# A gated recurrence and a highway layer: from running products on TensorE to a scan on VectorE, channels on the partitions

## The chip, the core and the metric

The kernel runs on one core of a Trainium2 chip. The core has a matrix engine (PE, TensorE), a vector engine (DVE, VectorE), an activation engine (ACT, ScalarE), a general engine (POOL, GpSimd) and a sync engine (SP) whose queue issues transfers. Each engine works through its own instruction list in order, and semaphores make one wait for another. SBUF is the on-chip memory of 128 partitions; PSUM is the smaller memory that TensorE writes, here eight banks of 2 KB in each partition. Sixteen DMA engines move data between HBM and SBUF. The metric is the device time in microseconds (us), as the median of the runs; less is better.

## The reference

There are B = 4 sequences of S = 6336 steps with D = 256 channels, in float32. Along a sequence each channel runs a gated recurrence; each of the 25344 results then goes through a highway layer.

```python
sig = 1.0 / (1.0 + np.exp(-f_logit))
f = lower_bound[None, None, :] + (1.0 - lower_bound[None, None, :]) * sig
i = 1.0 - f
for t in range(S):
    h = f[:, t] * h + i[:, t] * x[:, t]
    y[:, t] = h
...
H = np.maximum(x @ w_h, 0.0)
T = 1.0 / (1.0 + np.exp(-(x @ w_t + b_t)))
return (T * H + (1.0 - T) * x).astype(np.float32)
```

In the last three lines x is the recurrence's result y, with one row for each token. Each of f_logit, x and the output is 25344 x 256 float32, 25.95 MB.

## The kernel before

The kernel walks through the sequences in 50 chunks of 128 steps (the last one holds 64). A chunk has the 128 steps on the partitions and 4 x 256 = 1024 (sequence, channel) pairs along the free dimension, so 512 tokens. It is written as one straight loop body; a scheduler of the framework sets the order on each engine.

The recurrence is solved inside a chunk by products. ACT computes a Tanh of f_logit (L111), DVE turns it into f (L113, L114) and 1 - f (L120), POOL multiplies that with x (L123, the input b of the recurrence), and ACT takes the logarithm of f (L117). TensorE multiplies the logarithms with a triangular matrix of ones (L127), which sums them along the steps. ACT takes exp of the sum and of its negative (L131, L133): the product P of all f so far, and its inverse. DVE forms b/P (L136), TensorE sums it along the steps with the same triangular matrix and adds the last row of the chunk before through a one-hot matrix (L140, L143), and DVE multiplies by P (L146). This is y, with steps on the partitions. The next chunk's L143 needs this chunk's y, so the chunks form a chain.

For the highway layer the channels have to be on the partitions. TensorE transposes eight blocks of y (L153), DVE copies them out of PSUM (L154), TensorE multiplies with the two weight matrices (L164, L166), DVE takes the relu (L168), ACT a Tanh that stands for the sigmoid (L169), and DVE does the scaling and the three elementwise steps of the mix (L170, L174, L175, L177). TensorE transposes the result back (L183), DVE copies it out (L184), and POOL's queue stores it, cast from bf16 to float32 on the way (L186). The loads go through SP's queue (L107, L108), with three buffers each. The functions of ACT belong to different tables, which ACT_TABLE_LOAD rows bring in. Two of the PSUM pools hold one buffer of each tile and one holds two.

## Time and profile before

| what | value |
|---|---|
| median of 3 runs | 619.56 us (619.17 to 620.91) |
| profiled execution, span | 620.2 us |
| PE, DVE, ACT, POOL busy | 346.1, 471.4, 389.3, 165.8 us |
| ACT table loads | 95 of 1283 ns |
| HBM read, written | 52.95, 25.95 MB |
| mean granted TensorE clock | 0.674 |

The span is the time from the first to the last instruction of the one execution that the profiler recorded; that execution's own time and its span agree with the median to 0.1%. A row of the groups gives line, engine, operation, output and inputs with their shapes, the count, then after the bar the busy time and the mean duration of one in ns, and after the second bar how long the engine had been idle in front of it and which instruction ended that. A row of the timeline begins with its start and its duration in us. A row of the windows gives the stretch, its length, the busy time of PE, the weight loads, DVE, ACT and POOL with their counts, the granted TensorE clock, the share of the DMA engines and GB/s.

### The profile page before, as it was taken

The numbers are of one execution on the slowest core, as the hardware profiler recorded it, in microseconds if no ns is written. First come the engines' busy times: TensorE is split into PE (matmuls) and PEld (weight loads), VectorE is DVE, ScalarE is ACT, GpSimd is POOL, SyncE is SP. The second block draws the span as 40 slices with busy tenths as digits, with TensorE's granted clock in tenths as the row PEclk, the third lists the DMA queues.
The fourth block names the chain that finished last, engine by engine and source line by source line (L and its number), as shares of the span: only waits on it lengthen the run. The fifth ranks groups of instructions, "written<-read, shape, count | busy, mean of one in ns | idle before, by whom it ended". The sixth has DMA issues, their size and how long they took to land.

```text
span 620.2 us, 4764 instructions
## 1 busy us (share of the span) xinstructions
PE 346.1 (56%) x1473; PEld 164.6 (27%) x1498; DVE 471.4 (76%) x706; ACT 389.3 (63%) x395; POOL 165.8 (27%) x115
## 2 busy tenths in 40 slices
PE   0365545556456655645655665565565575566653
PEld 0122222222132232322323223222322232232321
DVE  1488899887887887878877877878878778766653
ACT  1976999786675675676676666666765574543010
POOL 3323354242232232223223223222322132120000
PEclk9976777776766666676676666666666666666655
DMA  8947568666646645744654564565463242122222
GB/s 151 289 135 204 136 169 234 175 181 158 136 103 146 159 102 135 165 107 106 174 126 103 148 157 101 135 157 115 108 161 87 68 100 54 34 50 52 61 40 51
DMA packets 79817, 78.69 MB, mean 127 GB/s; under 512 B 2736, under 2 KB 79792, under 8 KB 79792
## 3 DMA queue, kind: packets, MB, share of 16 engines
q1 hardware_dynamic: 52576, 51.91, 32.7%
q0 software_dynamic: 27216, 26.48, 19.1%
q8 instruction: 11, 0.18, 0.1%
q14 instruction: 14, 0.11, 0.1%
HBM read 52.95 MB, written 25.95 MB: 127 GB/s over the span
## 4 chain that ended last, share of the span: by engine, by line
PE 33%; issue 27%; DVE 18%; ACT 18%; DMA 2%; POOL 1%; SPq 0%; POOLq 0%; another core or an unknown queue 0%; ACTq 0%; DVEq 0%
PE H_ps L164 10%; PE T_ps L166 9%; ACT L117 6%; ACT lf L117 5%; PE Su_ps L140 5%; DVE yT L154 4%; PE Su_ps L143 4%; DVE out_pp L184 3%; DMA flg<-in_f_logit_dram 2%; ACT T_sb L169 2%; PE Lp_ps L127 2%; ACT invP L131 2%; DVE tmp L175 2%; DVE imf L120 2%; PE tps L183 1%
## 5 line engine op out<-in xcount | busy, mean ns | idle before, releaser
L123 POOL TENSOR_TENSOR bb<-imf,xt 128x1024 bf16<-128x1024 f16 x50 | 122.1, 2442 | 310.4 <-issue 288.6
L169 ACT ACTIVATE T_sb<-T_ps,bt_sb 128x512 bf16<-128x512 f32 x100 | 68.7, 687 | 172.6 <-PE T_ps L166 172.6
L164 PE MATMUL H_ps<-yT,wh_sb 128*128 128x512 bf16 x177 | 99.0, 576 | 77.8 <-DVE yT L154 76.4
L183 PE MATMUL tps<-ident,out_dp 128*128 128x128 bf16 x400 | 44.4, 278 | 151.6 <-DVE out_dp L177 151.6
L166 PE MATMUL T_ps<-yT,wt_sb 128*128 128x512 bf16 x200 | 110.3, 564 | 6.6 <-issue 5.1
L168 DVE TENSOR_SCALAR H_sb<-H_ps 128x512 bf16<-128x512 f32 x100 | 69.0, 690 | 48.8 <-PE H_ps L164 38.4
L113 DVE TENSOR_TENSOR ftile<-sig,nlb_tile 128x1024 f16<-128x1024 f16 x50 | 64.4, 1288 | 27.6 <-ACT lf L117 22.2
L183 PEld LDWEIGHTS <-out_dp 128*128 128x128 bf16 x400 | 32.6, 125 | 180.7 <-DVE out_dp L177 180.7
L186 POOL DMA_DIRECT2D out_dram<-out_pp x50 | 39.8, 796 | 139.1 <-DVE out_pp L184 136.8
L111 ACT ACTIVATE sig<-flg 128x1024 f16<-128x1024 f32 x50 | 52.7, 1056 | 27.9 <-DVE ftile L113 15.7
L140 PE MATMUL Su_ps<-uu,L_tile 128*128 128x512 bf16 x100 | 60.5, 607 | 7.8 <-DVE uu L136 7.6
L117 ACT ACT_TABLE_LOAD x47 | 60.3, 1283 | 0.8
L166 PEld LDWEIGHTS <-wt_sb 128*128 128x128 bf16 x200 | 25.8, 129 | 124.9 <-issue 122.9
L131 ACT ACTIVATE invP<-Lp_ps 128x1024 bf16<-128x1024 f32 x50 | 51.1, 1021 | 10.0 <-PE Lp_ps L127 9.7
L117 ACT ACTIVATE lf<-ftile 128x1024 bf16<-128x1024 f16 x50 | 52.6, 1056 | 1.2 <-DVE ftile L114 0.7
L170 DVE TENSOR_SCALAR T_sb<-T_sb 128x512 bf16<-128x512 bf16 x100 | 32.3, 324 | 26.5 <-ACT T_sb L169 26.2
L133 ACT ACTIVATE Pt<-Lp_ps 128x1024 bf16<-128x1024 f32 x50 | 50.8, 1016 | 2.4 <-DVE y_b L146 2.4
L111 ACT ACT_TABLE_LOAD x39 | 50.0, 1283 | 1.4 <-PEq L202 0.7
L127 PE MATMUL Lp_ps<-lf,L_tile 128*128 128x512 bf16 x99 | 36.3, 451 | 23.9 <-ACT lf L117 18.7
L184 DVE COPY out_pp<-tps 128x1024 bf16<-128x1024 bf16 x50 | 34.1, 683 | 15.1 <-PE tps L183 15.1
L164 PEld LDWEIGHTS <-wh_sb 128*128 128x128 bf16 x200 | 29.1, 146 | 43.2 <-issue 42.7
L175 DVE TENSOR_TENSOR tmp<-tmp,T_sb 128x1024 bf16<-128x1024 bf16 x50 | 38.3, 766 | 1.4
(39 smaller groups left out, 467.1 us busy)
## 6 DMA issues: line engine op xcount, KB each, us to landing
flg<-in_f_logit_dram SPq DMA_DIRECT2D x49, 512.0 KB, 6.2
xt<-in_x_dram SPq DMA_DIRECT2D x49, 512.0 KB, 3.8
out_dram<-out_pp POOLq DMA_DIRECT2D x49, 512.0 KB, 6.4
lb_tile<-in_lower_bound_dram POOLq DMA_DIRECT2D x1, 256.0 KB, 10.5
flg<-in_f_logit_dram SPq DMA_DIRECT2D x1, 256.0 KB, 3.8
xt<-in_x_dram SPq DMA_DIRECT2D x1, 256.0 KB, 3.4
out_dram<-out_pp POOLq DMA_DIRECT2D x1, 256.0 KB, 2.5
wh_sb<-in_moe_w_h_dram POOLq DMA_DIRECT2D x1, 128.0 KB, 11.6
```

Source lines behind the costliest of these rows:

```text
L111: nc.scalar.activation(sig, flg.rearrange("p b d -> p (b d)"), AF.Tanh, scale=0.5)
L113: nc.vector.tensor_mul(ftile, sig, nlb_tile)
L117: nc.scalar.activation(lf, ftile, AF.Ln)
L123: nc.gpsimd.tensor_mul(bb, imf, xt.rearrange("p b d -> p (b d)"))
L131: nc.scalar.activation(invP, Lp_ps, AF.Exp, scale=-1.0)
L140: nc.tensor.matmul(Su_ps[:, h * 512 : (h + 1) * 512], L_tile, uu[:, h * 512 : (h + 1) * 512], start=True, stop=(c == 0))
L164: nc.tensor.matmul(H_ps, wh_sb[:, ki, mi * P : (mi + 1) * P], yT[:, ki, :, :], start=st, stop=sp)
L166: nc.tensor.matmul(T_ps, wt_sb[:, ki, mi * P : (mi + 1) * P], yT[:, ki, :, :], start=st, stop=sp)
L168: nc.vector.tensor_relu(H_sb[:, mi], H_ps)
L169: nc.scalar.activation(T_sb[:, mi], T_ps, AF.Tanh, scale=0.5, bias=bt_sb[:, mi : mi + 1])
L183: nc.tensor.transpose(tps2[:, b, dh, :], out_dp[:, dh, b, :], ident)
L184: nc.vector.tensor_copy(out_pp, tps2.rearrange("p b dh q -> p b (dh q)"))
```

## The change

The whole body is rewritten. The work is now cut into units: one of 4 x 192 tokens (96 partitions by eight blocks), then 24 of 1024 consecutive tokens of one sequence (128 partitions by eight blocks), taken in turn over the four sequences. Loads and stores keep rows of 1 KB.

`gate` computes u = sigmoid(-f_logit) on ACT, `product` computes u * x on POOL in four parts. `decay_pe` and `b_pe` transpose u and u * x on TensorE so that channels lie on the partitions, 128 at a time (h = 0, 1). `decay_act` forms f = 1 - (1 - lower_bound) u on ACT. `scan` is one instruction of DVE that runs the recurrence along the free dimension, `tensor_tensor_scan`, with the last column of the unit before as its start. The factor 1 - lower_bound of the input is left out there and put into the weights and into two diagonal matrices (`diag`, `ndiag`), so the y of the kernel is the reference's y without that factor.

The highway layer stays with channels on the partitions: `z_pe` and `t_act` give T, `g_pe` adds w_h's product and the negative of y in PSUM, `d_dve` takes the maximum with the negative of y (relu(H) - y), `e_dve` multiplies by T. `o_pe` multiplies y by the diagonal and e by the identity as stationary operands, both accumulated into one PSUM tile: this transposes back to tokens on the partitions and adds the residual. `o_act` copies it out on ACT in four parts, and SP's queue stores it as float32.

The loop at the end writes the order of all engines by hand, as a pipeline over units: unit n is scanned while n-1 goes through the highway layer, n-2 goes out, n+1 is gated and n+2 is loaded. PSUM holds uT and bT (one bank each, one buffer), zp and gp (two banks each, one buffer) and op (one bank, two buffers).

The removed lines are the loop printed above. The added ones, without the blank ones, the setting up of the names and the unchanged launch:

```diff
+    rest = S % (NB * P)
+    assert rest % 2 == 0 and rest // 2 <= P and B * 2 == NB
+    units = [(rest // 2, [(b, 0, b * rest, rest) for b in range(B)])]
+    for s0 in range(rest, S, NB * P):
+        for b in range(B):
+            units.append((P, [(b, s0, 0, NB * P)]))
+    NU = len(units)
+    inp = ctx.enter_context(tc.tile_pool(name="inp", bufs=3))
+    mid = ctx.enter_context(tc.tile_pool(name="mid", bufs=3))
+    ypool = ctx.enter_context(tc.tile_pool(name="ypool", bufs=6))
+    ffn = ctx.enter_context(tc.tile_pool(name="ffn", bufs=2))
+    outp = ctx.enter_context(tc.tile_pool(name="outp", bufs=2))
+    ps1 = ctx.enter_context(tc.tile_pool(name="ps1", bufs=1, space=bass.MemoryType.PSUM))
+    ps2 = ctx.enter_context(tc.tile_pool(name="ps2", bufs=2, space=bass.MemoryType.PSUM))
+    st = [dict() for _ in range(NU)]
+    def load(n):
+        np_, segs = units[n]
+        lt = inp.tile([P, NB, D], FP32, tag="lt")
+        xt = inp.tile([P, NB, D], FP32, tag="xt")
+        for src, t in ((f_logit, lt), (x, xt)):
+            if len(segs) == 1:
+                b, s0, _, ln = segs[0]
+                nc.sync.dma_start(t, src[b, s0:s0 + ln, :].rearrange("(j p) d -> p j d", p=np_))
+            else:
+                t4 = t.rearrange("p (b j) d -> p b j d", j=2)
+                for j in range(2):
+                    nc.sync.dma_start(
+                        t4[:np_, :, j, :],
+                        src[:, j * np_:(j + 1) * np_, :].rearrange("b p d -> p b d"))
+        st[n]["lt"], st[n]["xt"] = lt, xt
+    load(0)
+    load(1)
+    ident_b = singles.tile([P, P], BF16, name="ident_b")
+    make_identity(nc, ident_b)
+    ident_h = singles.tile([P, P], FP16, name="ident_h")
+    make_identity(nc, ident_h)
+    lb = singles.tile([P, NH], FP32, name="lb")
+    bt = singles.tile([P, NH], FP32, name="bt")
+    w_raw = singles.tile([P, 2, NH, D], FP32, name="w_raw")
+    for h in range(NH):
+        for vec, t in ((lower_bound, lb), (moe_b_t, bt)):
+            nc.scalar.dma_start(t[:, h:h + 1], bass.AP(
+                tensor=vec.tensor, offset=vec.offset + h * P, ap=[[1, P], [1, 1]]))
+    for k, w in enumerate((moe_w_h, moe_w_t)):
+        nc.scalar.dma_start(w_raw[:, k], w.rearrange("(h p) o -> p h o", p=P))
+    cc = singles.tile([P, NH], FP32, name="cc")
+    nc.vector.tensor_scalar(cc, lb, -1.0, 1.0, op0=ALU.mult, op1=ALU.add)
+    ncc = singles.tile([P, NH], FP32, name="ncc")
+    nc.vector.tensor_scalar(ncc, lb, 1.0, None, op0=ALU.subtract)
+    w_sb = singles.tile([P, 2, NH, D], BF16, name="w_sb")
+    diag = singles.tile([P, NH, P], FP16, name="diag")
+    ndiag = singles.tile([P, NH, P], FP16, name="ndiag")
+    for h in range(NH):
+        for k in range(2):
+            nc.vector.tensor_scalar(w_sb[:, k, h], w_raw[:, k, h], cc[:, h:h + 1], None, op0=ALU.mult)
+        nc.vector.tensor_scalar(diag[:, h], ident_h, cc[:, h:h + 1], None, op0=ALU.mult)
+        nc.vector.tensor_scalar(ndiag[:, h], ident_h, ncc[:, h:h + 1], None, op0=ALU.mult)
+    def gate(n):
+        np_, _ = units[n]
+        u = mid.tile([P, NB, D], FP16, tag="u")
+        nc.scalar.activation(u[:np_], st[n]["lt"][:np_], AF.Sigmoid, scale=-1.0)
+        st[n]["u"] = u
+    def product(n):
+        np_, _ = units[n]
+        bv = mid.tile([P, NB, D], BF16, tag="bv")
+        for q in range(0, NB, 2):
+            nc.gpsimd.tensor_mul(bv[:np_, q:q + 2], st[n]["u"][:np_, q:q + 2], st[n]["xt"][:np_, q:q + 2])
+        st[n]["bv"] = bv
+    def decay_pe(n, h):
+        np_, _ = units[n]
+        uT = ps1.tile([P, NB * P], FP16, tag="uT")
+        for j in range(NB):
+            nc.tensor.transpose(uT[:, j * np_:(j + 1) * np_], st[n]["u"][:np_, j, h * P:(h + 1) * P], ident_h[:np_, :np_])
+        st[n]["uT"] = uT
+    def decay_act(n, h):
+        np_, _ = units[n]
+        N = NB * np_
+        if h == 0:
+            st[n]["f"] = mid.tile([P, NH, NB * P], FP16, tag="f", name="f")
+        nc.scalar.activation(st[n]["f"][:, h, :N], st[n]["uT"][:, :N], AF.Identity, scale=ncc[:, h:h + 1], bias=1.0)
+    def b_pe(n, h):
+        np_, _ = units[n]
+        bT = ps1.tile([P, NB * P], BF16, tag="bT")
+        for j in range(NB):
+            nc.tensor.transpose(bT[:, j * np_:(j + 1) * np_], st[n]["bv"][:np_, j, h * P:(h + 1) * P], ident_b[:np_, :np_])
+        st[n]["bT"] = bT
+    carry = {}
+    def scan(n, h):
+        if h == 0:
+            st[n]["y"] = ypool.tile([P, NH, NB * P], BF16, tag="y", name="y")
+        y = st[n]["y"]
+        for b, _, c0, ln in units[n][1]:
+            prev = carry.get((b, h))
+            nc.vector.tensor_tensor_scan(
+                y[:, h, c0:c0 + ln], st[n]["f"][:, h, c0:c0 + ln], st[n]["bT"][:, c0:c0 + ln],
+                0.0 if prev is None else prev, op0=ALU.mult, op1=ALU.add)
+            carry[b, h] = y[:, h, c0 + ln - 1:c0 + ln]
+    def halves(n):
+        N = NB * units[n][0]
+        return [(0, N // 2), (N // 2, N)]
+    def z_pe(n, m):
+        zp = ps1.tile([P, 2, 512], FP32, tag="zp")
+        y = st[n]["y"]
+        for ki in range(NH):
+            for i, (a, e) in enumerate(halves(n)):
+                nc.tensor.matmul(zp[:, i, :e - a], w_sb[:, 1, ki, m * P:(m + 1) * P], y[:, ki, a:e],
+                                 start=ki == 0, stop=ki == NH - 1)
+        st[n]["zp"] = zp
+    def t_act(n, m):
+        w = NB * units[n][0] // 2
+        if m == 0:
+            st[n]["t"] = ffn.tile([P, NH, 2, 512], BF16, tag="t", name="t")
+        nc.scalar.activation(st[n]["t"][:, m, :, :w], st[n]["zp"][:, :, :w], AF.Sigmoid, bias=bt[:, m:m + 1])
+    def g_pe(n, m):
+        gp = ps1.tile([P, 2, 512], FP32, tag="gp")
+        y = st[n]["y"]
+        for i, (a, e) in enumerate(halves(n)):
+            nc.tensor.matmul(gp[:, i, :e - a], ndiag[:, m], y[:, m, a:e], start=True, stop=False)
+        for ki in range(NH):
+            for i, (a, e) in enumerate(halves(n)):
+                nc.tensor.matmul(gp[:, i, :e - a], w_sb[:, 0, ki, m * P:(m + 1) * P], y[:, ki, a:e],
+                                 start=False, stop=ki == NH - 1)
+        st[n]["gp"] = gp
+    def d_dve(n, m):
+        w = NB * units[n][0] // 2
+        if m == 0:
+            st[n]["d"] = ffn.tile([P, NH, 2, 512], BF16, tag="d", name="d")
+        y2 = st[n]["y"][:, m, :2 * w].rearrange("p (i w) -> p i w", i=2)
+        nc.vector.scalar_tensor_tensor(st[n]["d"][:, m, :, :w], y2, ncc[:, m:m + 1], st[n]["gp"][:, :, :w],
+                                       op0=ALU.mult, op1=ALU.max)
+    def e_dve(n):
+        w = NB * units[n][0] // 2
+        e = mid.tile([P, NH, 2, 512], BF16, tag="e", name="e")
+        if w == 512:
+            nc.vector.tensor_mul(e, st[n]["d"], st[n]["t"])
+        else:
+            for m in range(NH):
+                nc.vector.tensor_mul(e[:, m, :, :w], st[n]["d"][:, m, :, :w], st[n]["t"][:, m, :, :w])
+        st[n]["e"] = e
+    def o_pe(n, q):
+        np_, _ = units[n]
+        w = NB * np_ // 2
+        op = ps2.tile([P, 2, D], FP32, tag="op")
+        y, e = st[n]["y"], st[n]["e"]
+        for jj in range(2):
+            j = 2 * q + jj
+            i, c = divmod(j * np_, w)
+            for h in range(NH):
+                o = op[:np_, jj, h * P:(h + 1) * P]
+                nc.tensor.matmul(o, y[:, h, j * np_:(j + 1) * np_], diag[:, h], start=True, stop=False)
+                nc.tensor.matmul(o, e[:, h, i, c:c + np_], ident_b, start=False, stop=True)
+        st[n]["op"] = op
+    def o_act(n, q):
+        np_, segs = units[n]
+        if q == 0:
+            st[n]["o"] = outp.tile([P, NB, D], FP32, tag="o", name="o")
+        o = st[n]["o"]
+        nc.scalar.copy(o[:np_, 2 * q:2 * q + 2], st[n]["op"][:np_])
+        if q == 3:
+            if len(segs) == 1:
+                b, s0, _, ln = segs[0]
+                nc.sync.dma_start(out_bsd[b, s0:s0 + ln, :].rearrange("(j p) d -> p j d", p=np_), o)
+            else:
+                o4 = o.rearrange("p (b j) d -> p b j d", j=2)
+                for j in range(2):
+                    nc.sync.dma_start(out_bsd[:, j * np_:(j + 1) * np_, :].rearrange("b p d -> p b d"),
+                                      o4[:np_, :, j, :])
+    def ok(n):
+        return 0 <= n < NU
+    for n in range(-2, NU + 2):
+        if ok(n + 2) and n + 2 > 1:
+            load(n + 2)
+        if ok(n):
+            b_pe(n, 0)
+            scan(n, 0)
+        if ok(n - 1):
+            g_pe(n - 1, 0)
+            z_pe(n - 1, 0)
+            d_dve(n - 1, 0)
+            t_act(n - 1, 0)
+        if ok(n + 1):
+            gate(n + 1)
+            product(n + 1)
+        if ok(n - 2):
+            o_pe(n - 2, 0)
+            o_act(n - 2, 0)
+            o_pe(n - 2, 1)
+            o_act(n - 2, 1)
+        if ok(n):
+            b_pe(n, 1)
+            scan(n, 1)
+        if ok(n + 1):
+            decay_pe(n + 1, 0)
+            decay_act(n + 1, 0)
+        if ok(n - 1):
+            g_pe(n - 1, 1)
+            z_pe(n - 1, 1)
+            d_dve(n - 1, 1)
+            t_act(n - 1, 1)
+        if ok(n + 1):
+            decay_pe(n + 1, 1)
+            decay_act(n + 1, 1)
+        if ok(n - 1):
+            e_dve(n - 1)
+        if ok(n - 2):
+            o_pe(n - 2, 2)
+            o_act(n - 2, 2)
+            o_pe(n - 2, 3)
+            o_act(n - 2, 3)
+        if ok(n - 2):
+            st[n - 2].clear()
```

More of the change, by code (lines that the diff above doesn't have):

```diff
@@ L7 @@
 from concourse._compat import with_exitstack
-from concourse.masks import make_upper_triangular, make_identity
+from concourse.masks import make_identity
 from concourse import _compat as _cc
@@ L16 @@
 AF = mybir.ActivationFunctionType
+ALU = mybir.AluOpType
 @with_exitstack
@@ L63 @@
-    nc.gpsimd.memset(r_hot, 0.0)
-    nc.gpsimd.affine_select(
-        out=r_hot, in_=r_hot,
-        compare_op=mybir.AluOpType.not_equal,
-        fill=1.0, base=-(P - 1), pattern=[[0, P]], channel_multiplier=1,
-    )
-    ident = singles.tile([P, P], BF16, name="ident")
-    make_identity(nc, ident)
-    ident32 = singles.tile([P, P], FP32, name="ident32")
-    make_identity(nc, ident32)
-    wh_sb = singles.tile([P, DH, D], BF16, name="wh_sb")
-    wt_sb = singles.tile([P, DH, D], BF16, name="wt_sb")
@@ L77 @@
-    nc.gpsimd.dma_start(wh_sb, moe_w_h.rearrange("(dh p) o -> p dh o", p=P))
-    nc.gpsimd.dma_start(wt_sb, moe_w_t.rearrange("(dh p) o -> p dh o", p=P))
-    bt_sb = singles.tile([P, DH], FP32, name="bt_sb")
-    for dh in range(DH):
-        bt_src = bass.AP(tensor=moe_b_t.tensor, offset=moe_b_t.offset + dh * P,
-                         ap=[[1, P], [1, 1]])
-        nc.sync.dma_start(bt_sb[:, dh : dh + 1], bt_src)
-    nc.vector.tensor_scalar_mul(bt_sb, bt_sb, 0.5)
-    wrk = ctx.enter_context(tc.tile_pool(name="wrk", bufs=2))
```

107 lines of the change are left out of this document (2 added, 105 removed).

## The prediction

> **What bounds the kernel now.** I read the page's first part, the queues and the chain of waits, then the groups by line, then the SP queue's waits and the timeline.
>
> ```profile
> span 620.2 us, 4764 instructions
> PE 346.1 (56%) x1473; PEld 164.6 (27%) x1498; DVE 471.4 (76%) x706; ACT 389.3 (63%) x395; POOL 165.8 (27%) x115
> ...
> HBM read 52.95 MB, written 25.95 MB: 127 GB/s over the span
> ...
> PE 33%; issue 27%; DVE 18%; ACT 18%; DMA 2%; POOL 1%; SPq 0%; POOLq 0%; another core or an unknown queue 0%; ACTq 0%; DVEq 0%
> ```
>
> No engine is full, and the chain passes through PE, DVE and ACT in turn: one chunk's operations wait for one another.
>
> ```profile
> L117 ACT ACT_TABLE_LOAD x47 | 60.3, 1283 | 0.8
> L111 ACT ACT_TABLE_LOAD x39 | 50.0, 1283 | 1.4 <-PEq L202 0.7
> ...
> L146 DVE TENSOR_TENSOR y_b<-Pt,Su_ps 128x1024 bf16<-128x1024 bf16 x25 | 30.2, 1208 | 2.2 <-PE Su_ps L143 2.2
> ```
>
> ```profile
> SPq L108 <- POOL bb L123: 368.4, 46, 14.4
> ```
>
> ```profile
> L146 DVE TENSOR_TENSOR y_a<-Pt,Su_ps x25: 1203/1205/1222, 25.4 to 577.2; 128x1024 bf16<-128x1024 bf16 x25
> L146 DVE TENSOR_TENSOR y_b<-Pt,Su_ps x25: 1203/1206/1222, 33.1 to 587.3; 128x1024 bf16<-128x1024 bf16 x25
> ```
>
> The 50 state updates of L146 start from 25.4 to 587.3 us: (587.3 - 25.4)/49 = 11.5 us a chunk of 512 tokens. In it DVE works 471.4/50 = 9.4 us and ACT 7.8 us, of which two table loads are over 2 us. The SP queue's 368.4 us are x loads waiting for a buffer that POOL reads: not a bound, since the transfers could run faster:
>
> ```profile
> 16.00:26.00 10.00, 2.88 (x6) 0.61 (x5) 4.93 (x8) 9.91 (x10) 4.32 (x3) 1.00 1.10 354
> ```
>
> The last number is GB/s, 354 over 10 us against a mean of 127.
>
> **The change, part by part.** A unit is now 1024 tokens of all 256 channels, so 24 whole units and one of 768 tokens. Tanh, Ln, two Exps, the running-sum matmuls and nearly all of DVE's 16-bit passes go. Per unit I count, with prices from these rows:
>
> ```profile
> L123 POOL TENSOR_TENSOR bb<-imf,xt 128x1024 bf16<-128x1024 f16 x50 | 122.1, 2442 | 310.4 <-issue 288.6 <-DVE imf L120 17.1 <-DVE uu L136 4.7
> L111 ACT ACTIVATE sig<-flg 128x1024 f16<-128x1024 f32 x50 | 52.7, 1056 | 27.9 <-DVE ftile L113 15.7 <-DMA flg<-in_f_logit_dram 12.2
> L131 ACT ACTIVATE invP<-Lp_ps 128x1024 bf16<-128x1024 f32 x50 | 51.1, 1021 | 10.0 <-PE Lp_ps L127 9.7
> L169 ACT ACTIVATE T_sb<-T_ps,bt_sb 128x512 bf16<-128x512 f32 x100 | 68.7, 687 | 172.6 <-PE T_ps L166 172.6
> L113 DVE TENSOR_TENSOR ftile<-sig,nlb_tile 128x1024 f16<-128x1024 f16 x50 | 64.4, 1288 | 27.6 <-ACT lf L117 22.2 <-ACT sig L111 5.5
> L136 DVE TENSOR_TENSOR uu<-bb,invP 128x1024 bf16<-128x1024 bf16 x50 | 34.2, 685 | 2.9 <-ACT invP L131 2.7
> ```
>
> ACT: gate, 2048 elements: at most 2 x 1.056 = 2.11; at least 1.06 + 1024 x (1.021 - 0.687)/512 = 1.73; I take 2.0. Each of two decay_act and two t_act: between 1.02 and 2 x 0.687 = 1.37, I take 1.1. Four o_act of 512: at most 0.69. Sum 2.0 + 4.4 + 2.7 = 9.1 us.
>
> POOL: product is four multiplies of 512 elements, the type of L123. Together at least two alone-standing ones, at most two mean ones and a fixed part:
>
> ```profile
> 14.57 2.13 POOL L123 TENSOR_TENSOR bb<-imf,xt 128x1024 bf16<-128x1024 f16 x1 [9.23 <-DVE imf L120]
> ```
>
> So 4.26 to 5.0; I take 4.8.
>
> DVE: two scans. The trace has none. The nearest row is L146 (one PSUM operand, 1.21 for 1024); a recurrence can't be cheaper than that, so no gain below it, and from above I take the slowest engine's 1024 elements, 2.45. I cost with 2.45, because each element waits for its predecessor. Two d_dve at L146's 1.21; e_dve 2 x 0.69 = 1.37, or up to 2 x 1.29 while POOL reads beside it, as L113 shows. Sum 4.9 + 2.4 + 1.4 = 8.7 us.
>
> The Trainium skill ("DVE: opcode table, instruction layouts, handler registers and perf-mode slots", section 6) says that the built-in scan runs at half throughput, which speaks against the change; by it a scan is an estimated 2.3 us, DVE 8.4 us and the result the same. No trace here shows a scan yet.
>
> PE: 32 transposes and 32 matmuls of 128 columns, 20 of 512: 4096 + 4096 + 10240 = 18432 columns.
>
> ```profile
> 242.89 0.63 PE L183 MATMUL tps<-ident,out_dp 128*128 128x128 bf16 x8 [2.58 <-DVE out_dp L177]
> ```
>
> ```profile
> 250.31 0.38 PE L164 MATMUL H_ps<-yT,wh_sb 128*128 128x512 bf16 x1
> 250.53 0.38 PE L166 MATMUL T_ps<-yT,wt_sb 128*128 128x512 bf16 x1
> ```
>
> At full clock 512 columns go each 0.22 us, with 0.16 until the end shows; eight transposes take 0.45 + 0.16. Sum 64 x 0.057 + 20 x 0.217 = 8.0 us, and twice that at half clock. What the mean clock would be follows from the windows of 3.41 us in which it changes (second column PE busy, third from the end the clock):
>
> ```profile
> 89.77:93.18 3.41, 2.93 (x19) 2.24 (x21) 2.45 (x5) 3.38 (x4) 2.87 (x2) 0.50 0.02 6
> 93.18:96.60 3.42, 2.98 (x13) 0.99 (x11) 3.36 (x7) 2.99 (x5) 0.01 (x1) 1.00 0.99 220
> ...
> 110.25:113.66 3.41, 0.68 (x8) 0.34 (x7) 3.38 (x8) 3.39 (x4) 0.00 (x0) 1.00 0.16 36
> 113.66:117.08 3.42, 2.42 (x17) 1.65 (x16) 3.14 (x5) 3.38 (x4) 3.08 (x2) 0.50 0.36 129
> 117.08:120.49 3.41, 3.41 (x9) 1.21 (x9) 2.55 (x6) 1.79 (x3) 0.15 (x1) 0.50 0.73 210
> ```
>
> ```profile
> 72.70:76.12 3.42, 2.14 (x10) 0.69 (x8) 3.35 (x7) 3.09 (x5) 0.00 (x0) 1.00 1.42 386
> 76.12:79.53 3.41, 1.93 (x20) 1.15 (x19) 3.41 (x8) 3.39 (x5) 1.58 (x1) 1.00 0.37 120
> ```
>
> After 2.93 busy of 3.41 (86%) at half clock the next window is at full clock; after 2.42 (71%) it isn't. After 0.68 (20%) at full clock it falls; after 2.14 (63%) it doesn't. The new PE would be saturated at half clock (16 us of work), so it rises, and at full clock it is busy for some 70%, so it mostly stays.
>
> Transfers: 1.05 MB each of f_logit, x and output a unit, 3.15 MB at 354 GB/s = 8.9 us. They hide behind anything longer. The store moves from POOL's queue to SP's, where it waits for the last o_act, and the loads of unit n+3 stand behind it. In the walk below they issue 1.5 us into iteration n+1; gate(n+3) reads f_logit some 13 us later, and store and f_logit need 2.1/0.354 = 5.9 us and about 2 to land. Covered, by about 5 us; without that cover the 8.9 us come onto the path.
>
> Now the iteration. PSUM has one buffer each for uT, bT, zp and gp, so the written order decides. On PE, g and z of unit n-1 stand behind b_pe(n,0), which waits for POOL's product(n); on ACT, gate(n+1) stands behind t_act(n-1,0), which waits for z; and product(n+1) waits for gate(n+1). That is a closed loop, once an iteration: gate 2.0 + product 4.8 + b_pe 0.45 + g 6 x 0.217 = 1.30 + z 4 x 0.217 = 0.87 + its end 0.16 + t_act 1.1 + four handovers, 0.2 = **10.9 us** (bounds 9.7 and 11.8). A handover is short:
>
> ```profile
> 250.94 0.69 ACT L169 ACTIVATE T_sb<-T_ps,bt_sb 128x512 bf16<-128x512 f32 x1 [0.82 <-PE T_ps L166]
> ```
>
> (the matmul before it ends at 250.53 + 0.38 = 250.91.) Beside the loop, from b_pe's start at 0: scan to 3.1, d 4.3, second scan 6.8, then DVE waits for g(n-1,1), which stands behind decay_pe(n+1,0), which waits for the gate at 5.9; d ends 9.0, e behind t_act(n-1,1) at 11.1. So DVE could repeat each 10.5 us, ACT each 9.3, and the loop's 10.9 is late last. It is longer than the transfers.
>
> Start: the first f_logit reaches ACT thus:
>
> ```profile
> 7.36 1.06 ACT L111 ACTIVATE sig<-flg 128x1024 f16<-128x1024 f32 x1 [5.34 <-DMA flg<-in_f_logit_dram]
> ```
>
> gate(0) at 7, product(0) to 13.9, product(1) to 18.7, then b, g, z (768 columns), t_act, gate(2) to 24. Then 22 iterations to gate(24). Tail: product and b_pe 5.5, scan, d, scan 6.1, d and e of unit 23 2.6, d, g, z, t of unit 24 4.7, e 1.4, o_pe and four o_act 3.4, store about 5.3 (a read of 512 KB takes 3.8 by the row below, 1.5 more for the second half): 29.
>
> ```profile
> xt<-in_x_dram SPq DMA_DIRECT2D x49, 512.0 KB, 3.8
> ```
>
> Sum 24 + 22 x 10.9 + 29 = 293, and 4 for single windows at half clock: **297 us**. That is of the profiled execution, whose span before, 620.2, is 0.1% over the median 619.56; I forecast the median the same.
>
> **The rivals.** (B) The clock falls often. For it: the gaps stand next to each other if gate and product come late, and the mean now is 0.674:
>
> ```profile
> core 0: 620.2 us, clock 0.674
> ```
>
> Against: the windows above. At half clock throughout PE's 16 us a unit set the pace: 53 + 22 x 16 = 405; at a mean clock of 0.75 the loop is 10.9 + 2.6/2 = 12.2 with PE 10.7 us busy, 321. The Trainium skill ("TensorE: Matmul & The Clock Gate", Part 4) says that transposes don't count as busy for the gate; then 4096 of the 18432 columns would not count and (B), with its 321, would be likelier. The trace disagrees:
>
> ```profile
> 89.89 1.03 PE L183 MATMUL tps<-ident,out_dp 128*128 128x128 bf16 x8 [4.98 <-DVE out_dp L177]
> 90.72 1.06 PE L153 MATMUL tps<-ident,y_b 128*128 128x128 bf16 x8
> ```
>
> 16 transposes fill 1.7 us of the 2.93 after which the clock rose.
>
> (C) The functions of ACT (Sigmoid, Identity, copy) don't share a table: now Tanh and Ln alternate for 86 loads of 1.283. With five switches a unit ACT has 9.1 + 6.4 = 15.5 us: 53 + 22 x 15.5 = 394.
>
> (D) A scan costs more than 2.45: then DVE sets the pace, 2s + 3.8; at s = 4.4, 12.6 us and 330.
>
> (E) Slower than before: the scan isn't pipelined, each element waiting for the whole pass of the one before. What a pass costs is bounded by the fixed part of an instruction:
>
> ```profile
> L168 DVE TENSOR_SCALAR H_sb<-H_ps 128x512 bf16<-128x512 f32 x100 | 69.0, 690 | 48.8 <-PE H_ps L164 38.4 <-remote 9.7
> ```
>
> From 512 elements to L146's 1024 an element costs (1.208 - 0.690)/512 = 1.01 ns, so 0.17 us is fixed. If each element waited a fourteenth of that, 12 ns, a scan would take 12.4 us, an iteration 2 x 12.4 + 3.8 = 28.6, the kernel 53 + 22 x 28.6 = 682. It decides from (620 - 53)/22 = 25.8 = 2s + 3.8, s = 11 us. Against: that is nine times L146.
>
> (F) All prices at their low ends: 51 + 22 x 9.7 = 264.
>
> **How the numbers follow.** The forecast (264 to 313 by the bounds) 0.55; B 0.2; C 0.05; D 0.1; E 0.04; below 264, 0.06. The range 265 to 370 leaves out F, the worst of B, C and E, about 0.2. Within 0.3% is 618 to 621 (what a measurement here can tell from no change): 0.01, between D and E; slower 0.04; faster 0.95.
>
> **What would show it.** Right: POOL's first multiply of a unit starts right behind gate, b_pe(n,0) idles for POOL, t_act idles for z, units follow each other by about 11 us; scans of 1.2 to 2.5 us; one or two table loads in all; a mean clock over 0.85; DMA near 290 GB/s. Wrong: scans above 4 us with DVE full; PE full at a clock near 0.5; gate waiting for f_logit's transfer.

## The result, and the profile after

The changed kernel takes **314.4 us** (median of 4 runs, 312.08 to 317.42) beside 619.96 us for the kernel before (4 runs, 619.17 to 620.91). The ratio is **0.506, 95% interval 0.503 to 0.508**. The forecast was 297 us with a range of 265 to 370, so the time lies in the range and 17 us above the forecast. One of the four runs, at 317.42 us, was in a slower state: the ratio and the differences below leave it out, and the median without it is 313.4 us. The profiled execution took 312.08 us, with a span of 310.0 us at a granted clock of 0.969.

The page's first part, the queues and the chain of waits of the kernel after:

```profile
span 310.0 us, 5042 instructions
PE 222.9 (72%) x2100; PEld 145.1 (47%) x2100; DVE 207.8 (67%) x142; ACT 203.2 (66%) x226; POOL 120.0 (39%) x108
...
HBM read 52.43 MB, written 25.95 MB: 253 GB/s over the span
...
POOL 29%; issue 27%; PE 15%; DVE 13%; ACT 6%; DMA 6%; SPq 1%; POOLq 1%; DVEq 0%; ACTq 0%
```

The work shrank as the change says: DVE from 471.4 us in 706 instructions to 207.8 in 142, ACT from 389.3 to 203.2. Still no engine is full. The kernel before already had a chain that passed from engine to engine; it has one again, with POOL, 39% busy, now its largest part.

The groups of instructions by line, shapes apart (the number behind the bar is the busy time, then the mean ns of one, then the idle time before them and what ended it):

```profile
L153 DVE TENSOR_TENSOR_SCAN y<-f,y,bT 128x1024 bf16<-128x1024 f16 x48 | 112.5, 2344 | 43.5 <-PE bT L142 37.6 <-ACT o L225 5.0 <-ACT u L114 0.8
L193 DVE SCALAR_TENSOR_TENSOR d<-y,ncc,gp 128x1024 bf16<-128x1024 bf16 x48 | 60.9, 1268 | 30.7 <-PE gp L184 30.6
L175 ACT ACTIVATE t<-zp,bt 128x1024 bf16<-128x1024 f32 x48 | 53.4, 1113 | 51.2 <-PE zp L167 51.0
L114 ACT ACTIVATE u<-lt 128x2048 f16<-128x2048 f32 x24 | 46.0, 1918 | 0.6 <-DMA lt<-in_f_logit_dram 0.6
L200 DVE TENSOR_TENSOR e<-d,t 128x2048 bf16<-128x2048 bf16 x24 | 31.0, 1291 | 3.4 <-ACT t L175 2.9
L153 DVE TENSOR_TENSOR_SCAN y<-f,bT 128x192 bf16<-128x192 f16 x8 | 3.8, 535 | 7.7 <-PE bT L142 7.7
L114 ACT ACT_TABLE_LOAD x1 | 1.3, 1283 | 6.7 <-DMA lt<-in_f_logit_dram 6.7
```

One scan of 1024 tokens takes 2.344 us, one of 192 tokens 0.535: (2344 - 535)/(1024 - 192) = 2.17 ns an element. One table load is left of 95, of which Tanh and Ln alone had 86. The gate waits for f_logit's transfer for 0.6 us in the whole run after the first load.

POOL's own row of the timeline (start, duration, and in brackets the idle time before and its releaser) shows the pace, since each row is one unit's four multiplies:

```profile
18.72 4.51 POOL L121 TENSOR_TENSOR bv<-u,xt 128x512 bf16<-128x512 f16 x4 [2.74 <-ACT u L114]
26.10 4.83 POOL L121 TENSOR_TENSOR bv<-u,xt 128x512 bf16<-128x512 f16 x4 [2.87 <-ACT u L114]
...
43.28 4.53 POOL L121 TENSOR_TENSOR bv<-u,xt 128x512 bf16<-128x512 f16 x4 [3.82 <-ACT u L114]
...
64.41 5.50 POOL L121 TENSOR_TENSOR bv<-u,xt 128x512 bf16<-128x512 f16 x4 [5.53 <-ACT u L114]
...
283.64 4.51 POOL L121 TENSOR_TENSOR bv<-u,xt 128x512 bf16<-128x512 f16 x4 [7.67 <-ACT u L114]
```

The multiplies of unit 2 start at 26.10 and those of unit 24 at 283.64: (283.64 - 26.10)/22 = **11.7 us a unit** where 10.9 was predicted. It isn't even: 8.2 us over the three units from 18.72 to 43.28, and (283.64 - 64.41)/18 = 12.18 over the last eighteen. Four of these, of 12.8 to 13.7 us, hold a window of 3.4 us with the granted clock near 0.5; in the 3.4 us before it, PE had been busy for only 0.9 to 1.7 us each time. They take 13.1 us in the mean beside 11.9 for the other fourteen, so these windows cost about 5 us by this estimate.

What stands between two gates is seen in the timeline of one such iteration, cut to the rows that hand over to each other:

```profile
222.28 1.92 ACT L114 ACTIVATE u<-lt 128x2048 f16<-128x2048 f32 x1
...
224.28 4.52 POOL L121 TENSOR_TENSOR bv<-u,xt 128x512 bf16<-128x512 f16 x4 [7.12 <-PE gp L184]
...
228.86 0.28 PE L142 MATMUL bT<-ident_b,bv 128*128 128x128 bf16 x2 [0.83 <-POOL bv L121]
...
229.25 2.35 DVE L153 TENSOR_TENSOR_SCAN y<-f,y,bT 128x1024 bf16<-128x1024 f16 x1 [3.73 <-PE bT L142]
...
231.65 0.61 PE L142 MATMUL bT<-ident_b,bv 128*128 128x128 bf16 x8 [0.99 <-DVE y L153]
232.09 0.38 PE L167 MATMUL zp<-y,w_sb 128*128 128x512 bf16 x1
...
232.51 1.11 ACT L175 ACTIVATE t<-zp,bt 128x1024 bf16<-128x1024 f32 x1 [2.52 <-PE zp L167]
...
233.52 1.06 ACT L225 COPY o<-op 128x512 f32<-128x512 f32 x2
234.46 1.93 ACT L114 ACTIVATE u<-lt 128x2048 f16<-128x2048 f32 x1
```

The gate and its handover take 2.00 us, the multiplies 4.58 to the last transposes, those 0.39 to the scan, the scan 2.40. Only then can PE transpose the second half (the one buffer bT is read by the scan): 0.44. Behind that stands the last matmul of zp, 0.42 with its end; t_act 1.01; two output copies, 0.94; then the next gate. The sum is 12.18 us. In the source the order is another one: z stands ahead of b_pe(n,1), and gate ahead of the output copies. The order that ran isn't the order that was written, so what the section on the change says, that the loop writes the order of all engines by hand, does not hold for this kernel. Nor does each iteration end alike: in the one before (gates at 210.34 and 222.28) z was done early, and behind b_pe(n,1) came output matmuls and two copies. The scan and b_pe(n,1) stand ahead of the gate in both.

### The profile page after: what moved, and what is told of

It is laid out like the page before. It is cut to its first block, busy times and chain, and to the rows that moved or that the text cites. A ratio compares the mean times of both kernels' runs of the same rounds, so it can differ in the third digit from the quotient of the medians.

```text
span 310.0 us, 5042 instructions
## 1 busy us (share of the span) xinstructions
PE 222.9 (72%) x2100; PEld 145.1 (47%) x2100; DVE 207.8 (67%) x142; ACT 203.2 (66%) x226; POOL 120.0 (39%) x108
## 3 DMA queue, kind: packets, MB, share of 16 engines
HBM read 52.43 MB, written 25.95 MB: 253 GB/s over the span
## 4 chain that ended last, share of the span: by engine, by line
POOL 29%; issue 27%; PE 15%; DVE 13%; ACT 6%; DMA 6%; SPq 1%; POOLq 1%; DVEq 0%; ACTq 0%
POOL bv L121 29%; DVE y L153 10%; DMA xt<-in_x_dram 5%; PE gp L184 4%; PE zp L167 4%; ACT u L114 3%; PE bT L142 3%; DVE d L193 2%; ACT o L225 2%; PE gp L181 1%; DMA lt<-in_f_logit_dram 1%; PE op L216 1%; ACT t L175 1%; PE op L217 1%; PE uT L128 1%
## 5 line engine op out<-in xcount | busy, mean ns | idle before, releaser
L121 POOL TENSOR_TENSOR bv<-u,xt 128x512 bf16<-128x512 f16 (+1 forms) x100 | 118.9, 1220 | 167.6 <-ACT u L114 131.3
L153 DVE TENSOR_TENSOR_SCAN y<-f,y,bT 128x1024 bf16<-128x1024 f16 x48 | 112.5, 2344 | 43.5 <-PE bT L142 37.6
L175 ACT ACTIVATE t<-zp,bt 128x1024 bf16<-128x1024 f32 (+1 forms) x50 | 55.2, 1104 | 51.2 <-PE zp L167 51.0
L193 DVE SCALAR_TENSOR_TENSOR d<-y,ncc,gp 128x1024 bf16<-128x1024 bf16 (+1 forms) x50 | 62.9, 1257 | 31.2 <-PE gp L184 31.2
L136 ACT ACTIVATE f<-uT,ncc 128x1024 f16<-128x1024 f16 (+1 forms) x50 | 55.4, 1108 | 26.9 <-PE uT L128 26.2
L225 ACT COPY o<-op 128x512 f32<-128x512 f32 (+1 forms) x100 | 53.9, 590 | 16.2 <-PE op L217 15.2
L184 PE MATMUL gp<-y,w_sb 128*128 128x512 bf16 (+1 forms) x200 | 57.2, 384 | 9.9 <-DVE y L153 9.9
L216 PE MATMUL op<-diag,y 128*128 128x128 f16 (+1 forms) x400 | 56.5, 228 | 2.1 <-ACT o L225 1.4
L167 PE MATMUL zp<-y,w_sb 128*128 128x512 bf16 (+1 forms) x200 | 56.1, 384 | 0.0
L217 PE MATMUL op<-ident_b,e 128*128 128x128 bf16 (+1 forms) x400 | 56.0, 227 | 0.1
```

Source lines behind the costliest of these rows:

```text
L121: nc.gpsimd.tensor_mul(bv[:np_, q:q + 2], st[n]["u"][:np_, q:q + 2], st[n]["xt"][:np_, q:q + 2])
L153: nc.vector.tensor_tensor_scan(y[:, h, c0:c0 + ln], st[n]["f"][:, h, c0:c0 + ln], st[n]["bT"][:, c0:c0 + ln], 0.0 if prev is None else pre ...
L167: nc.tensor.matmul(zp[:, i, :e - a], w_sb[:, 1, ki, m * P:(m + 1) * P], y[:, ki, a:e], start=ki == 0, stop=ki == NH - 1)
L175: nc.scalar.activation(st[n]["t"][:, m, :, :w], st[n]["zp"][:, :, :w], AF.Sigmoid, bias=bt[:, m:m + 1])
L184: nc.tensor.matmul(gp[:, i, :e - a], w_sb[:, 0, ki, m * P:(m + 1) * P], y[:, ki, a:e], start=False, stop=ki == NH - 1)
L193: nc.vector.scalar_tensor_tensor(st[n]["d"][:, m, :, :w], y2, ncc[:, m:m + 1], st[n]["gp"][:, :, :w], op0=ALU.mult, op1=ALU.max)
```

## The experiments

The theory after this reading: **the unit's time is that of a loop across engines, and the scheduler's order of each engine's list adds 1.2 us to it.** Its rivals, taken up one by one below: that POOL's multiplies, the scans, the transfers or DVE as a whole set the pace whatever the order.

**The written order.** Each engine's instructions are chained, by edges that order the list and add no wait, as the source has them.

```
+    last = {}
+    for ins in list(nc.cur_bb.bb.instructions):
+        if ins.engine in last:
+            tc.add_manual_dep(ins, last[ins.engine].name, mybir.DependencyInfo(
+                mybir.DependencyClass.NoSync, mybir.DependencyReason.DATA), reason="written order")
+        last[ins.engine] = ins
```

> Only the order is changed: every engine issues its instructions in the order in which the loop writes them, as the prediction assumed; the scheduler's own order in the changed kernel differs. Theory A (a closed loop sets the pace, in the changed kernel gate, product, b_pe, scan, b_pe, then z_pe and t_act or o_pe and o_act, and gate again, 12.2 us a unit): in the written order the loop is the predicted one without the scan; with the prices now measured, 1.92 + 4.52 + 0.45 + 1.30 + 0.87 + 0.16 + 1.1 + 0.2 = 10.5 us a unit and some 284 us in all (270 to 292). Rival B (the transfers set the pace, slower with stores among the loads): no change, 310 to 318. Rival C (DVE's own work sets the pace): no change, 310 to 318.

Measured: 281.73 us (280.66 to 282.32), ratio 0.453 (0.451 to 0.454). The chain of waits in order of time (start, duration, engine, what and line) and one row of the timeline:

```profile
167.87 1.91 ACT u L114
...
169.84 4.54 POOL bv L121 x4
...
174.42 0.28 PE bT L142 x2
174.71 0.43 PE gp L181 x2
175.14 0.86 PE gp L184 x4
176.00 0.65 PE zp L167 x3
...
177.91 1.91 ACT u L114
```

```profile
176.90 1.11 ACT L175 ACTIVATE t<-zp,bt 128x1024 bf16<-128x1024 f32 x1 [1.19 <-PE gp L184]
```

This is the prediction's loop, member by member: gate, product, b_pe, g, z, then t_act to 176.90 + 1.01 (the chain shows PE's output matmuls there, which run beside it) and the next gate right behind: 177.91 - 167.87 = 10.04 us. It was predicted at 10.9 with bounds of 9.7 and 11.8. The only edit is the order, and it is worth 313.4 - 281.7 = 32 us. About 5 of these are the windows at half clock; here the units follow each other by 10.05 us from the third on, and ahead of the tail there is one such window, near 30 us. So the scheduler's order is shown to be the cause of the excess.

**Gate and product one iteration earlier,** in the scheduler's order; the loads move with them, and the pools get a fourth buffer.

```
-    inp = ctx.enter_context(tc.tile_pool(name="inp", bufs=3))
-    mid = ctx.enter_context(tc.tile_pool(name="mid", bufs=3))
+    inp = ctx.enter_context(tc.tile_pool(name="inp", bufs=4))
+    mid = ctx.enter_context(tc.tile_pool(name="mid", bufs=4))
-    for n in range(-2, NU + 2):
-        if ok(n + 2) and n + 2 > 1:
-            load(n + 2)
+    for n in range(-3, NU + 2):
+        if ok(n + 3) and n + 3 > 1:
+            load(n + 3)
-        if ok(n + 1):
-            gate(n + 1)
-            product(n + 1)
+        if ok(n + 2):
+            gate(n + 2)
+            product(n + 2)
```

> gate and product run two units ahead of the scan and not one, the loads three, with four buffers in place of three; the scheduler orders as it likes. Theory A: product has a whole unit of time before b_pe reads it, the loop is cut, and the next limit is the transfers (3.15 MB at 354 GB/s, 8.9 us) or ACT and DVE (8.5 us each) with some waits: 9.3 to 10.5 us a unit, 250 to 280 us. Rival B (transfers) and rival C (DVE): no change, 308 to 318.

Measured: 276.21 us (275.14 to 278.56), ratio 0.444 (0.442 to 0.447). The product has left the chain, and this loop took over:

```profile
169.25 1.28 DVE e L200
170.53 2.26 DVE y L153
172.79 1.18 DVE d L193
...
175.34 1.03 PE gp L184 x4
...
176.80 0.46 PE uT L128 x8
177.28 1.11 ACT f L136
178.39 1.01 ACT t L175
...
179.43 1.22 DVE e L200
```

From e to e it is 179.43 - 169.25 = 10.2 us: the scan and d on DVE, d frees the one gp buffer, then g with output matmuls between, z, decay_pe, decay_act and t_act, for which e waits. Taking 6.5 us of gate and product off the loop gave only 12.18 - 10.15 = 2 us a unit, because the next loop is that close behind.

**Half the product.** Only every second block of 128 tokens is multiplied; b_pe transposes each computed block twice, so PE's work stays.

```
-            nc.gpsimd.tensor_mul(bv[:np_, q:q + 2], st[n]["u"][:np_, q:q + 2], st[n]["xt"][:np_, q:q + 2])
+            nc.gpsimd.tensor_mul(bv[:np_, q:q + 1], st[n]["u"][:np_, q:q + 1], st[n]["xt"][:np_, q:q + 1])
-            nc.tensor.transpose(bT[:, j * np_:(j + 1) * np_], st[n]["bv"][:np_, j, h * P:(h + 1) * P], ident_b[:np_, :np_])
+            nc.tensor.transpose(bT[:, j * np_:(j + 1) * np_], st[n]["bv"][:np_, j - j % 2, h * P:(h + 1) * P], ident_b[:np_, :np_])
```

> product multiplies only every second block of 128 tokens, and b_pe transposes each computed block twice; half of the input of the recurrence is left out of the computation, all else has its size. POOL's part falls from 4.5 to about 2.4 us a unit. Theory A: product lies in the loop, so 22 x 2.1 = 46 us less, about 268, unless another limit comes first (the transfers at 8.9 us a unit): 255 to 280. Rivals B and C: no change, 310 to 318.

Measured: 281.66 us (2 runs), ratio 0.453 (0.451 to 0.454). POOL's rows of the timeline:

```profile
211.55 2.57 POOL L121 TENSOR_TENSOR bv<-u,xt 128x256 bf16<-128x256 f16 x4 [8.30 <-ACT u L114]
222.42 2.57 POOL L121 TENSOR_TENSOR bv<-u,xt 128x256 bf16<-128x256 f16 x4 [8.30 <-ACT u L114]
```

The unit went from 12.18 to 222.42 - 211.55 = 10.87 us, though the product became 4.52 - 2.57 = 1.95 us shorter. The product was on the loop, since shortening it by itself made the kernel 313.4 - 281.7 = 32 us faster. But the expectation counted the whole cut as gain and missed by 14 us: at 10.87 another loop (d, scan, e, scan, g, d, and g and d once more) ends last, and DVE's share of the chain is 36%.

**No scan.** The scan is replaced by one add of the same operands; the recurrence is left out.

```
-            nc.vector.tensor_tensor_scan(
-                y[:, h, c0:c0 + ln], st[n]["f"][:, h, c0:c0 + ln], st[n]["bT"][:, c0:c0 + ln],
-                0.0 if prev is None else prev, op0=ALU.mult, op1=ALU.add)
+            nc.vector.tensor_tensor(
+                y[:, h, c0:c0 + ln], st[n]["f"][:, h, c0:c0 + ln], st[n]["bT"][:, c0:c0 + ln],
+                op=ALU.add)
```

> The scan is replaced by one elementwise addition of the same operands: the recurrence is left out of the computation, the shapes stay. Each falls from 2.34 to about 1.2 us. Theory A: one of a unit's two scans is in the loop, so 22 x 1.14 = 25 us less, about 289 (280 to 295). Rival C (DVE's work): both count, 22 x 2.3 = 50 us less, about 263. Rival B: no change, 310 to 318.

Measured: 289.43 us (2 runs), ratio 0.465. The number was met for a partly wrong reason: the add took 0.69 us, not the 1.2 expected, so 1.65 us a scan were taken away, and of one such saving a unit (22 x 1.65 = 36 us) 313.4 - 289.4 = 24 arrived, at most 3.3 of it from the two scans of the tail. So a scan stands on the loop of the kernel after, where the prediction's loop has none.

**Both: gate ahead, and the written order.** The edits of the first two experiments together.

> gate, product and the loads one unit earlier, and the written order on every engine. In the written order a DVE loop is left: scan, d, scan, d, then e, which waits for the second t_act; that stands on ACT behind z, gate, two o_act and a decay_act (0.6 to 10.3 us after b_pe's start in the prediction's walk): 9.7 us a unit against 10.15 of the run with gate ahead alone, so 22 x 0.45 = 10 us less than its 276: 266 (262 to 272). Rival B (the transfers are the limit by now: 3.15 MB at the 325 to 340 GB/s seen in the busy slices of the two runs before, 9.3 to 9.7 us): 257 to 266, the same within what can be told.

Measured: 258.08 us (257.18 to 259.36), ratio 0.416 (0.414 to 0.418), a unit of 9.09 us: 8 us under my own expectation. The chain is now gate, two o_act, decay_act, decay_pe, o_pe, b_pe, g, z, t_act. It carries most of ACT's work in a row, then PE's. The time fell into what the rival by transfers expected as well; half of x settles that below.

**The gate later in the iteration.** As before, with the gate and product written behind e_dve.

```
-        if ok(n + 2):
-            gate(n + 2)
-            product(n + 2)
         if ok(n - 2):
             o_pe(n - 2, 0)
...
         if ok(n - 1):
             e_dve(n - 1)
+        if ok(n + 2):
+            gate(n + 2)
+            product(n + 2)
```

> As the run with gate ahead and the written order, and gate and product are written behind e_dve, so that ACT's second t_act no longer stands behind the gate. Theory A (waits set the pace): t_act 1.9 us earlier, e follows d, DVE runs nearly without a gap, 8.6 to 9.0 us a unit, 245 to 253 us. Rival B (the transfers are the limit): 9.3 to 9.7 us a unit, no better than 257 to 266, with the gate waiting for f_logit's transfer.

Measured: 245.61 us (244.65 to 246.18), ratio 0.396 (0.394 to 0.397). The stretch of 100 us (length, busy time of PE, PEld, DVE, ACT and POOL, granted clock, DMA share, GB/s) and the chain:

```profile
100.00:200.00 100.00, 92.06 (x954) 64.21 (x969) 94.71 (x58) 91.74 (x106) 53.50 (x48) 1.00 1.07 367
```

```profile
168.51 1.91 ACT u L114
170.41 0.48 ACT o L225
...
172.04 0.45 PE bT L142 x8
...
175.13 0.47 ACT t L175
...
177.14 1.91 ACT u L114
```

A unit is 8.63 us. DVE is busy for 94.7%, PE for 92%, ACT for 91.7%, and the transfers run at 367 GB/s, so the profile alone doesn't say which sets the pace. Two runs take one of them away each.

**Half of x.** The kernel just shown, with half of x not loaded (the product reads the loaded half twice).

```
-                nc.sync.dma_start(t, src[b, s0:s0 + ln, :].rearrange("(j p) d -> p j d", p=np_))
+                hb = NB // 2 if src is x else NB
+                nc.sync.dma_start(t[:, :hb], src[b, s0:s0 + hb * np_, :].rearrange("(j p) d -> p j d", p=np_))
-            nc.gpsimd.tensor_mul(bv[:np_, q:q + 2], st[n]["u"][:np_, q:q + 2], st[n]["xt"][:np_, q:q + 2])
+            nc.gpsimd.tensor_mul(bv[:np_, q:q + 2], st[n]["u"][:np_, q:q + 2], st[n]["xt"][:np_, q % 4:q % 4 + 2])
```

> The run with the gate last, which takes 8.63 us a unit, has two limits next to each other: DVE is busy for 8.2 of them, and 3.15 MB in 8.63 us is 365 GB/s. Here half of x is not loaded (product uses the other half twice, so that part of the input is left out of the computation): 2.62 MB a unit. If the transfers set the pace: 2.62/0.365 = 7.2, so DVE's 8.2 to 8.5 remains: 3 to 9 us less than 245.6, 236 to 243. If DVE with its two short waits sets it: no change, 244 to 247.

Measured: 245.23 us (2 runs), ratio 0.395. The same stretch:

```profile
100.00:200.00 100.00, 92.06 (x954) 64.21 (x969) 94.68 (x58) 91.74 (x106) 53.66 (x48) 1.00 0.94 306
```

A sixth of the traffic is gone and every busy time is the same to 0.2 us. Transfers don't set this pace.

**No scan, in the kernel of the later gate:** that kernel with the edit of the run without scans.

> The run with the gate last, each scan replaced by one elementwise addition of the same operands (the recurrence is left out of the computation): DVE 2 x 1.14 = 2.3 us less a unit. If DVE sets the pace at 8.63: the next limits are ACT (7.9 us of work), PE (8.0) and the transfers (8.6 at the 365 GB/s seen, 8.1 at the 386 of the busiest slices): 8.1 to 8.6 us a unit, 233 to 245 us with a shorter tail. If the transfers set it: 240 to 245, only the tail shorter.

Measured: 243.38 us (2 runs), ratio 0.392. A timeline row of the add, and the stretch:

```profile
176.21 0.68 DVE L153 TENSOR_TENSOR y<-f,bT 128x1024 bf16<-128x1024 f16 x1
```

```profile
100.00:200.00 100.00, 92.09 (x959) 64.43 (x974) 58.16 (x58) 90.96 (x107) 54.31 (x48) 1.00 1.07 366
```

DVE falls from 94.7% to 58% busy and the kernel gains 2 us. The time lies in both of the ranges expected, so the unit decides: it stays at 8.63 us (the multiplies start at 169.29 and 177.92). So DVE at 95% wasn't what set the pace either. What is left, by the chain of the run with the later gate, is a loop between ACT and PE, in which the output copy, behind the gate, frees the PSUM buffer that o_pe waits for, and b_pe, g and z stand behind o_pe.

**The gate behind the last output copies.** If that loop is the cause, the copies should go ahead of the gate.

```
-        if ok(n + 2):
-            gate(n + 2)
-            product(n + 2)
         if ok(n - 2):
             o_pe(n - 2, 2)
             o_act(n - 2, 2)
             o_pe(n - 2, 3)
             o_act(n - 2, 3)
+        if ok(n + 2):
+            gate(n + 2)
+            product(n + 2)
```

> In the run with the gate last, neither half of x less nor the scans away changed the unit's 8.63 us, so a loop of PE and ACT is left: t_act 1.0, decay_act 1.0, gate 1.9, o_act 0.5 (which frees one of the two op buffers), o_pe 0.9, b_pe 0.45, decay_pe 0.45, g and z 2.2, t_act again: 8.4 and handovers. Here gate and product are written behind the last two o_act, so that the gate is not in front of them. If that loop sets the pace it loses 1.9 and gains 0.5, and ACT's and PE's own work, 8.0 us a unit, is next: 8.1 to 8.5 us, 234 to 242 us. If it is something else: 244 to 247, no change.

Measured: **237.0 us** (5 runs, 236.55 to 237.96), ratio **0.3815 (0.3807 to 0.3823)**, the fastest of all.

```profile
100.00:200.00 100.00, 98.58 (x1037) 68.72 (x1035) 98.49 (x62) 95.93 (x110) 54.97 (x49) 1.00 1.09 383
```

```profile
174.74 4.53 POOL L121 TENSOR_TENSOR bv<-u,xt 128x512 bf16<-128x512 f16 x4 [3.69 <-ACT u L114]
182.95 4.53 POOL L121 TENSOR_TENSOR bv<-u,xt 128x512 bf16<-128x512 f16 x4 [3.68 <-ACT u L114]
```

A unit is 182.95 - 174.74 = 8.21 us, with PE and DVE over 98% busy. DVE's own sum, by the steps in the chain of the run with the gate ahead (scan 2.26, d 1.18, e 1.22), is 2 x 2.26 + 2 x 1.18 + 1.22 = 8.1 us. No reordering has much left to gain here.

**The residual undone.** The last part of the change by itself: in the scheduler's order, o_pe only transposes, and two more DVE instructions add the residual.

```
+        for m in range(NH):
+            y2 = st[n]["y"][:, m, :2 * w].rearrange("p (i w) -> p i w", i=2)
+            nc.vector.scalar_tensor_tensor(e[:, m, :, :w], y2, cc[:, m:m + 1], e[:, m, :, :w],
+                                           op0=ALU.mult, op1=ALU.add)
-                nc.tensor.matmul(o, y[:, h, j * np_:(j + 1) * np_], diag[:, h], start=True, stop=False)
-                nc.tensor.matmul(o, e[:, h, i, c:c + np_], ident_b, start=False, stop=True)
+                nc.tensor.matmul(o, e[:, h, i, c:c + np_], ident_b, start=True, stop=True)
```

> One part of the change undone in the changed kernel, in the scheduler's order: the residual is added by two more DVE instructions of 128x1024 a unit (about 1.26 us each), and o_pe only transposes, 16 matmuls of 128 columns less (0.9 us of PE a unit). Theory A: PE's part of the loop shrinks by at most 0.4 us, DVE's grows: DVE's work becomes 11.0 of 12.2 us a unit and e comes 2.5 us later; 314 at best and up to 22 x 2.5 = 55 us more, about 335. If PE's work counted more than DVE's: 295 to 305.

Measured: 351.17 us (350.84 to 351.5, 2 runs), ratio 0.566 (0.564 to 0.567). A group of POOL's and a timeline row of the two added instructions:

```profile
L121 POOL TENSOR_TENSOR bv<-u,xt 128x512 bf16<-128x512 f16 (+1 forms) x100 | 156.2, 1591 | 167.2 <-ACT u L114 143.2 <-PE gp L184 14.1 <-DMA xt<-in_x_dram 9.9
```

```profile
181.21 4.16 DVE L206 SCALAR_TENSOR_TENSOR e<-y,cc,e 128x1024 bf16<-128x1024 bf16 x2
```

It lies within its range but above the 335 expected: the adds took 1.87 us each in the mean (2.08 in the row shown) instead of the 1.26 of the like-shaped d, and the mean multiply on POOL 1.59 instead of 1.22. So in this order, adding the residual in the transposing matmuls is worth 351.2 - 313.4 = 38 us. Part of that is a contention between POOL and DVE that the term of d doesn't show. The granted clock was lower too, 0.913 beside 0.969, and no run separates the two parts.

## Why the prediction was right, and where it was not

**The work per unit was right.** ACT was costed at 9.1 us a unit and measured 203.2/24.75 = 8.2 (the gate 1.92 for 2.0; t_act 1.11 and decay_act 1.12 for 1.1; two output copies 1.06 for "at most" 2 x 0.69). DVE was costed at 8.7 and measured 207.8/24.75 = 8.4 (scan 2.34 for 2.45, d 1.27 for 1.21, e 1.29 for 1.37). POOL was costed at 4.8 and measured 118.9/24.75 = 4.8, by the busy time of its group in the next fence.

```profile
L121 POOL TENSOR_TENSOR bv<-u,xt 128x512 bf16<-128x512 f16 (+1 forms) x100 | 118.9, 1220 | 167.6 <-ACT u L114 131.3
```

**The scan** fell between its ends, at 96% of the upper one: costing an operation that the trace does not show by the slowest engine's row was right here. The Trainium skill ("DVE: opcode table, instruction layouts, handler registers and perf-mode slots", section 6) says half throughput, and the trace agrees: 2.17 ns an element beside the 1.01 ns that the prediction worked out for a DVE pass over PSUM.

**Start and tail were nearly right.** product(2) starts at 26.1, where gate(2) was to end at 24; the tail from the last product's start was 310.0 - 283.64 = 26.4 instead of 29.

**The step that failed is "PSUM has one buffer each for uT, bT, zp and gp, so the written order decides".** The first half is right: those single buffers make the loops in every run above. The second isn't: a scheduler orders each engine's list, as the kernel before had one too, and I took the source's order for the issued one. It put the fourth matmul of z behind b_pe(n,1), which waits for the scan to release bT, and two output copies ahead of the gate. By the terms: g 1.30 and z 0.87 + 0.16, together 2.33, became scan 2.40, b_pe 0.44 and the last of z 0.42, together 3.26; the copies add 0.94; the rest came out 0.6 shorter than priced; 12.18 in place of 10.9 us in the iteration shown. Averaged over all units it is 11.7, and 22 x 0.8 = 18 us. With the start +2, the tail -3, the 4 us set aside for half-clock windows (whose cost is inside the 18), and 312.08 - 310.0 = 2 between span and time, that is 297 + 18 + 2 - 3 - 4 + 2 = 312, the profiled execution's time.

The run in the written order shows this to be the cause: there the predicted loop stands in the chain and the time is 281.7. The prediction's prices were thus too high by about 0.9 us an iteration (10.04 against 10.9: the product's 4.54 for 4.8, the last transposes' 0.28 for 0.45, the gate's 1.91 for 2.0, t_act's 1.01 for 1.1, and the rest in ends and handovers), which hid half of what the order cost (11.7 - 10.04 = 1.7). That 297 came within 17 us is thus in part luck: the loop that it assumed, when it runs, gives 282. The time also lies just above the upper end of the sum's own bounds (264 to 313), and in the stated range because that was drawn wider for the rivals.

**The rivals.** B, a clock that falls often, did not come: 0.969 over the span, with the four windows above and one in the tail, near the 4 us set aside. The runs that load PE more have more (1.00 in the windows above), while the run with the residual on DVE has less (0.913). The windows of the kernel before had pointed that way. The Trainium skill ("TensorE: Matmul & The Clock Gate", Part 4) says that transposes don't count; the 321 us that B would give by it weren't seen, but no run here separates whether the other matmuls alone would have held the clock. The prediction's "the trace disagrees" was too strong: in the timeline of the kernel before, the window ahead of the rise holds 1.7 us of transposes and 1.25 us of other matmuls, and the one without a rise 1.3 and 1.1 us, so both counts put them in the same order. C fell with one table load. D and E fell with the scan's 2.34. "Below 264" is what other orders of the same work reach: F's 9.7 us loop was taken as the low end because only this loop was considered.

**What was to show it** came true in most of its signs: POOL idles for the gate (131.3 of 167.6 us in the fence above), t_act for z (51.0 of 51.2), the scan for b_pe. These signs fit the loop that ran as well as the one predicted, so they couldn't tell the two apart; the distance of the units (12.18 instead of 11) and the order of the rows between two gates could. The sign of the transfers was off, 253 GB/s over the span where near 290 was expected. "Covered, by about 5 us" held nearly: after the first load the gate waits 0.6 us for f_logit in the whole run, and the product once, for 0.9 us, for x (it starts at 53.31, the gate's end being at 52.43).

## What to carry to other kernels

When no engine is full, walk the loop: which instruction waits for which, once round all the engines, and what else stands in each engine's list between them. Take that list from the order that is issued, not from the source, since the same work took 314 us in the scheduler's order, 282 in the written one, and 237 in a better written one with a fourth buffer. A long stage that only feeds later units (gate and product, 6.5 us) belongs an iteration further ahead, behind everything on its engine that frees a buffer for the others; and after each cut look for the next loop, as shortening by 6.5 us gave 2.

## What the runs showed of the hardware

**POOL and DVE slow each other** when both work on two operands in SBUF. Two rows of the kernel after, in which nothing else on DVE reads two operands there:

```profile
76.41 5.55 POOL L121 TENSOR_TENSOR bv<-u,xt 128x512 bf16<-128x512 f16 x4 [6.50 <-ACT u L114]
...
77.47 1.23 DVE L200 TENSOR_TENSOR e<-d,t 128x2048 bf16<-128x2048 bf16 x1
```

Undisturbed, the product takes 4.53 us, 1.13 for each multiply (the timeline rows of the fastest kernel), and e 1.22 to 1.28 (the chain of the run with the gate ahead). In these rows POOL alone is longer, by 1 us. In the written order it is e alone: 1.63 us in the mean, with the product at 4.52. In the run with both edits (gate ahead, written order) both are longer, 1.376 us a multiply and 1.510 for e in the mean; in the run with the residual on DVE, the multiply takes 1.591 and the adds 1.87. The kernel before has both cases as well: at 98.28 its POOL multiply takes 4.25 us and L113 beside it 0.69, at 158.53 the multiply takes 2.45 and L113 1.96. That they share a way to SBUF is an inference; the rows show only that one of them, or both, take longer where they overlap.

**A bf16 operand in PSUM doesn't slow DVE's add.** It took 0.68 us for 1024 elements, as long as the 0.685 of the pass over SBUF in the kernel before, while the pass with a float32 operand in PSUM took 1.21.

**The transfers** ran at 383 GB/s over 100 us in the fastest kernel, above the 354 that the prediction took for what they could do.
